# The last chunk's second product in 26 block products, and the last output row stored in two parts

## The chip, the cores and the metric

The kernel runs on one core of a Trainium2 chip. The metric is the device time of one execution in microseconds (us), as the median over runs. Traces come from one profiled execution; times in them are in us from the start of its span. Engines are named as in the profile: PE is TensorE, PEld its weight loads, DVE is VectorE, ACT is ScalarE, POOL is GpSimd, SP is SyncE, which issues most DMAs.

## The reference

Four batches, eight heads, 768 time steps and head dimension 40 go through an mLSTM cell, a recurrence with gates, whose output is rearranged to 3072 rows of 320 columns. Those go through two dense layers with a quick GELU between them:

```python
    h = x @ w_in                                  # 3072x320 @ 320x2048
    g = h * (1.0 / (1.0 + np.exp(-1.702 * h)))
    return (g @ w_out).astype(np.float32)         # 3072x2048 @ 2048x320
```

Everything is fp32. Only the end of this is touched by the change: `g @ w_out` for the last 128 time steps of all four batches, that is, for 512 rows.

## The kernel before

The time axis is cut into six chunks (`w` from 0 to 5, `NW = 6`) of 128 steps. For each chunk the cell is computed in its chunked form (scores, values, carried state); then the two dense layers follow for the chunk's 4 x 128 rows. Chunk `w`'s second layer is interleaved by hand with the cell of chunk `w + 1`, so the last chunk's second layer stands alone at the end. The order of the instructions on each engine is the order in which the program emits them (`tc.manual_schedule()`); each engine works its own queue in that order, and waits on semaphores where it needs another's result. Tiles in a pool (`bufs` of them for a tag) are used in turn.

**First layer, `up_fast` (L496).** It is called twice per chunk, for `j = 0` and `j = 4`; each call makes eight of the 16 blocks of 128 hidden units, `g`. It uses Winograd's form of Strassen's scheme (seven products of 2x2 blocks for eight) on the first 256 of the 320 inputs, and ordinary products (L546) for the other 64. Four sums of the inputs go ahead on DVE (L506 to L509); then, if given, the function `between` is called, which can emit other work to the queues at that place. PE runs the products (L518) into the banks `p_u` and `p_v`; ACT copies some out (L523); DVE adds others into `g` (L526); ACT applies the GELU (L530). L546 writes into the banks that the first four additions of L526 read, so it comes after them.

**Second layer, `down_fast` (L602).** For the chunk's rows of two batches at a time (`c` 0 and 1) it uses the same scheme once more: the hidden dimension is cut in two halves of eight blocks, the output columns in two halves of 160 (`DH`), the rows in two batches. Each of its seven products is a chain of eight hidden blocks into one PSUM bank of `ps_m` (L615); each fp32 block shows as two matmul records in the trace. DVE copies a product (L618) or adds it (L620) into the output tile `o_sb`. The sums of weights that it needs, `t1`, `t2`, `t4` and a changed `w01`, are made once, in chunk 1 (`weight_sums`, L585). The sums of hidden blocks are made per chunk by `hidden_sums` (L596) on DVE, in the room of `big` and `xs`; some in place in `g`. A row block of 128 x 320 is stored with one DMA on SP's queue when both its halves are final (L624).

The driver loop runs `up_fast(w, 0)`, then `up_fast(w, 4)`, with hidden sums emitted after each, and then the list of 14 second-layer products. At the end of the last chunk nothing else is left: POOL has nothing to do there at all.

Names that the change uses: `k_st`, `v_st`, `state`, `q_bl`, `k_bl`, `eo` and the `wt`, `kT`, `qT` tiles belong to the cell and are free once chunk 5's cell is done. `ps_a` has four PSUM banks, `ps_x` two and `ps_m` two. `V`, `A`, `G`, `T` are DVE, ACT, POOL and PE.

Of the kernel before, what the change touches and what calls it, by code (L numbers as in the profile page):

```python
# [22 lines left out]
L = 128  # L23
# [11 lines left out]
def kernel(  # L35
# [24 lines left out]
    DH = DM // 2  # L60
# [25 lines left out]
    eo = {}  # L86
# [409 lines left out]
    def up_fast(w, j, between=None):  # L496

        x = xT[w].rearrange("p c b t -> p c (b t)")  # L500
        ts = slice(0, W // 2), slice(W // 2, W)
        b00, b10, b01, b11 = (x[:, c, t] for t in ts for c in range(2))
        bt1, bt2, bt4 = (xs[:, i * 256:(i + 1) * 256] for i in range(3))
        js = range(j, j + 4)
        if j == 0:
            V.tensor_tensor(out=bt1, in0=b01, in1=b00, op=OP.subtract)  # L506
            V.tensor_tensor(out=bt2, in0=b11, in1=bt1, op=OP.subtract)
            V.tensor_tensor(out=b01, in0=b11, in1=b01, op=OP.subtract)
            V.tensor_tensor(out=bt4, in0=b10, in1=bt2, op=OP.subtract)  # L509
        if between:  # L510
            between()
        chain = {k: (ps_m if k - j < 2 else ps_x).tile([128, W], FP, tag="mx"[(k - j) // 2], name="p_u") for k in js}
        other = {k: ps_a.tile([128, W], FP, tag="a", name="p_v") for k in js}
        g = {k: hidden_of(w, k) for k in js}

        def product(p, t, a, b, first=False):
            for k in js:
                T.matmul(p[k][:, ts[t]], a[:, k // 2, k % 2 * 128:(k % 2 + 1) * 128], b, start=first,  # L518
                         stop=True, skip_group_check=True)

        def take(i, t):
            for k in js:
                A.copy(out=g[k][i][:, ts[t]], in_=chain[k][:, ts[0]])  # L523

        def add(k, i, t, p, pt):
            V.tensor_tensor(out=g[k][i][:, ts[t]], in0=p[k][:, ts[pt]], in1=g[k][i][:, ts[t]], op=OP.add)  # L526

        def gelu(k, i, t, src=None):
            dst = g[k][i][:, ts[t]]
            A.activation(out=dst, in_=dst if src is None else src, func=AF.Gelu_apprx_sigmoid)  # L530

        product(chain, 0, a00, b00, True)
        take(0, 0)
        product(other, 0, a01, b10, True)
        product(chain, 0, as2, bt2)
        take(0, 1)
        product(other, 1, as4, b11)
        product(chain, 0, a10, b01)
        take(1, 1)
        product(chain, 1, as1, bt1)  # L540
        for k in js:
            add(k, 0, 1, chain, 1)
        for k in js:
            for i, p in enumerate((other, chain)):
                r = slice(i * 64, i * 64 + 64)
                T.matmul(p[k], w_in_x[r, k, :], x[r, 2, :], start=False, stop=True, skip_group_check=True)  # L546

        for k in js:
            add(k, 1, 1, chain, 1)
            add(k, 0, 0, other, 0)  # L550
# [83 lines left out]

    def attention(w):
        if w > 1:

            return [[(columns, w)], [(weights, w, 0), (weights, w, 1)],  # L640
                    [(scores, w, 0), (hidden_sums, w - 1, 1, range(4), 3), (scores, w, 1), (weights, w, 2),
                     (weights, w, 3)],
                    [(values, w, 0), (values, w, 1), (scores, w, 2), (scores, w, 3)] +
                    [(scale, w, b) for b in (0, 1) if w + 1 < NW],
                    [(seam, w, 0), (seam, w, 1), (last_values, w)], [(carry, w)] if w + 1 < NW else [],
                    [(seam, w, 2)], [(seam, w, 3)]]
        return [[(columns, w)], [(weights, w, 0), (weights, w, 1)], [(scores, w, 0), (scores, w, 1)],
                [(weights, w, 2), (gates_out, w), (values, w, 0, 1), (scale, w, 0), (scale, w, 1)],
                [(weights, w, 3), (scores, w, 2), (scores, w, 3)], [(seam, w, 0), (seam, w, 1)],
                [(last_values, w)], [(seam, w, 2), (seam, w, 3)], [(new_states, w), (carry, w)]]  # L650
# [96 lines left out]
    def next_keys():  # L747
# [3 lines left out]
        transposes(w + 1, 0)  # L751
        transposes(w + 1, 1)

    for w in range(NW):
        more = w + 1 < NW
        for j in range(NF // 2):
            if w == 0 and j == 0:
                for pair_ in range(2):
                    for i, g in enumerate(hidden_of(0, pair_)):
                        A.activation(out=g, in_=first[pair_][i], func=AF.Gelu_apprx_sigmoid)  # L760
                    if pair_ == 0:
                        weights_in(0)
            elif w == 0 and j % 2 == 0:
                weights_in(j // 2)
                up(j, j == 2)
            elif w and j % 4 == 0:
                up_fast(w, j, next_keys if more and j == 0 else None)
            if w == 0 and j == 0:
                load_blocks(1, 0)
                spread(1)  # L770
                load_blocks(1, 1)
            if w == 1 and j == 3:
                weight_sums(3)
            if more:
                if w and j == 0:
                    load(w + 1, "o")
                if j == 4:
                    load(w + 1, "v")
                    if w:
                        spread(w + 1)  # L780
                    else:
                        fetch(17)
                        load(1, "o")
                if j == (4 if w else 6):
                    load(w + 1, "k")
                if w and j == 3:
                    for b in range(2, 4):
                        transposes(w + 1, b)
            if w and j in (3, 7):
                hidden_sums(w, 0, (j // 4 * 2, j // 4 * 2 + 1), 1, 2)  # L790
                if j == 3:
                    hidden_sums(w, 0, (0, 1), 3, 4)
        side = attention(w + 1) if more else []
        if w == 0:

            blocks = [(lambda b=b, n=n: down(w, b, n)) for ns in ((0, 1), (2,), (3,)) for b in range(B) for n in ns]
            stops = (0, 1, 5, 6, 8, 10, 12, 14, 15)
        else:
            blocks = down_fast(w, 0) + down_fast(w, 1)
            stops = (0, 1, 2, 4, 8, 10, 11, 12)  # L800
        for i, block in enumerate(blocks):
            if w == 0:
                weights_in(4 + i)
                if i == 0:
                    load_gates(2)
                if i == 2:
                    for b in range(B):
                        transposes(1, b, slice(0, 1))
                    first_sums((0, 1))
                    for b in range(B):  # L810
                        transposes(1, b, slice(1, 2))
                if i == 10:
                    load_blocks(2)
            elif w + 2 < NW and i == 0:
                load_gates(w + 2)
                load_blocks(w + 2)
            block()
            if i in stops and side:
                run(side.pop(0))
            if w == 1 and i == 1:  # L820
                weight_sums(2)
            if w:
                for at, c, *what in ((0, 0, (2, 3), 3), (1, 0, (2, 3), 4), (1, 1, range(4), 1),
                                     (5, 1, range(2), 2), (6, 1, range(2, 4), 2), (7, 1, range(4), 4)):
                    if i == at:
                        hidden_sums(w, c, *what)
                if i == 2 and not more:
                    hidden_sums(w, 1, range(4), 3)
            elif i == 11:
                weight_sums(0)  # L830
                weight_sums(1)
# [30 lines left out]
```

## Time and profile before

| what | value |
|---|---|
| median of 12 runs | 485.89 us |
| lowest and highest run | 485.77 and 486.84 us |
| the profiled execution, own time | 485.89 us |
| its span | 484.2 us |
| PE busy in the span | 478.1 us (99%) |
| DVE busy | 343.0 us (71%) |
| ACT busy | 220.7 us (46%) |
| POOL busy | 60.5 us (12%) |
| last chunk's first layer on PE | 418.65 to 450.75 us |
| last chunk's second layer on PE | 450.75 to 481.19 us |
| last DVE addition ends, last store is issued | 481.53, 481.56 us |

The busy time of PE is the modelled occupancy of a pipelined engine. The shares are averages over the whole span; the change touches the stages from 418.65 us on, and the first of them is where work of the second is prepared. DVE's and POOL's shares in those stages are what counts, not their shares of the span.

### The profile page before, as it was taken

How to read it: one execution, taken by the hardware profiler on the slowest of the kernel's cores; microseconds unless marked ns; L12 is line 12 of the kernel's file. 1: busy time of each engine (PE TensorE's matmuls, PEld its weight loads, DVE VectorE, ACT ScalarE, POOL GpSimd, SP SyncE). 2: the span in 40 equal slices, each digit the busy share in tenths (PEclk: the TensorE clock that was granted, in tenths of full speed). 3: DMA queues.
4: the chain of work that ended last, by engine and by line, in shares of the span. 5: the costliest groups of instructions: out<-in, count | busy, mean ns of one | idle time of the engine just before them, and what ended most of it. 6: DMA issues, size and time to landing. Idle time of an engine off the chain costs nothing. (4 is left out here: it accounts for less than half of the span.)

```text
span 484.2 us, 10432 instructions
## 1 busy us (share of the span) xinstructions
PE 478.1 (99%) x4072; PEld 396.9 (82%) x4072; DVE 343.0 (71%) x853; ACT 220.7 (46%) x575; POOL 60.5 (12%) x101
## 2 busy tenths in 40 slices
PE   8999999999999999999999999999999999999997
PEld 5874457777879999788999877999877999977997
DVE  8788878887978965667766677686576786254831
ACT  7667673603649302467600466900374920255300
POOL 3020001520001420000341000332000120000000
PEclk9999999999999999999999999999999999999999
DMA  9999689954997000997000896200492000000000
GB/s 127 190 257 343 86 199 198 165 76 73 194 174 79 7 30 28 213 156 81 3 29 15 124 248 66 29 28 3 85 260 22 1 15 16 28 1 0 1 27 28
DMA packets 175953, 44.87 MB, mean 93 GB/s; under 512 B 164352, under 2 KB 169504, under 8 KB 175904
## 3 DMA queue, kind: packets, MB, share of 16 engines
q1 hardware_dynamic: 175328, 43.55, 49.1%
q8 instruction: 32, 0.52, 0.5%
q10 hardware_dynamic: 576, 0.66, 0.4%
q14 instruction: 17, 0.14, 0.1%
HBM read 40.17 MB, written 4.01 MB: 91 GB/s over the span
## 5 line engine op out<-in xcount | busy, mean ns | idle before, releaser
L615 PE MATMUL p_out<-w_out_sb,g 128*128 128x160 f32 x480 | 69.8, 301 | 0.0
L615 PEld LDWEIGHTS p_out<-w_out_sb,g 128*128 128x128 f32 x480 | 66.3, 190 | 0.9
L405 ACT COPY xT<-p_x 128x384 f32<-128x384 f32 x24 | 10.8, 484 | 120.2 <-PE p_x L404 107.1
L526 DVE TENSOR_TENSOR g<-p_u,g 128x256 f32<-128x256 f32 x80 | 33.7, 424 | 44.6 <-PE p_u L518 35.0
L523 ACT COPY g<-p_u 128x256 f32<-128x256 f32 x120 | 43.1, 377 | 43.5 <-PE p_u L518 39.3
L530 ACT ACTIVATE g<-g 128x256 f32<-128x256 f32 x120 | 42.3, 424 | 39.3 <-DVE g L526 39.3
L336 POOL TENSOR_SCALAR_AFFINE_SELECT wt<-wt 128x1024 f32<-128x1024 f32 x20 | 22.8, 1138 | 239.8 <-ACT wt L334 239.0
L620 DVE TENSOR_TENSOR o_sb<-o_sb,p_out 128x160 f32<-128x160 f32 x70 | 21.4, 318 | 42.2 <-PE p_out L615 41.8
L334 ACT ACTIVATE wt<-wt,cols 128x128 f32<-128x128 f32 x160 | 47.8, 392 | 0.0
L518 PE MATMUL p_u<-xT,w_in_sb 128*128 128x256 f32 x160 | 38.9, 382 | 0.0
L518 PE MATMUL p_u<-xs,big 128*128 128x256 f32 x160 | 37.9, 379 | 0.0
L546 PE MATMUL p_v<-xT,w_in_x 64*128 64x512 f32 x80 | 37.0, 602 | 0.0
L546 PE MATMUL p_u<-xT,w_in_x 64*128 64x512 f32 x80 | 37.0, 602 | 0.0
L566 PE MATMUL p_out<-w_out_sb,g 128*128 128x320 f32 x128 | 36.3, 437 | 0.0
L352 DVE TENSOR_TENSOR wt<-p_s,wt 128x512 f32<-128x512 f32 x48 | 30.4, 683 | 8.1 <-POOL wt L336 6.7
L615 PE MATMUL p_out<-t,big 128*128 128x160 f32 x240 | 35.5, 301 | 0.0
L518 PEld LDWEIGHTS p_u<-xT,w_in_sb 128*128 128x128 f32 x160 | 29.6, 190 | 5.4 <-DVE o_sb L620 1.5
L518 PEld LDWEIGHTS p_u<-xs,big 128*128 128x128 f32 x160 | 30.0, 190 | 4.6 <-ACT g L523 0.2
L615 PEld LDWEIGHTS p_out<-t,big 128*128 128x128 f32 x240 | 33.3, 190 | 0.2
L566 PEld LDWEIGHTS p_out<-w_out_sb,g 128*128 128x128 f32 x128 | 23.7, 190 | 9.9 <-issue 0.5
L526 DVE TENSOR_TENSOR g<-p_v,g 128x256 f32<-128x256 f32 x80 | 29.8, 415 | 0.0
L546 PEld LDWEIGHTS p_v<-xT,w_in_x 64*128 64x128 f32 x80 | 14.2, 186 | 16.0 <-issue 16.0
(172 smaller groups left out, 857.4 us busy)
## 6 DMA issues: line engine op xcount, KB each, us to landing
wt<-m_row SPq DMA_DIRECT2D x20, 512.0 KB, 6.7
v_st<-in_v_dram SPq DMA_DIRECT2D x5, 640.0 KB, 8.9
eo<-in_o_gate_dram SPq DMA_DIRECT2D x5, 640.0 KB, 5.5
k_st<-in_k_dram SPq DMA_DIRECT2D x5, 640.0 KB, 11.3
out_dram<-o_sb SPq DMA_DIRECT2D x20, 160.0 KB, 1.8
big<-in_moe_w_in_dram SPq DMA_DIRECT2D x5, 512.0 KB, 7.0
k_bl<-in_k_dram SPq DMA_DIRECT2D x40, 64.0 KB, 2.7
q_bl<-in_q_dram SPq DMA_DIRECT2D x40, 64.0 KB, 2.6
```

The costliest lines, as they stand in the source:

```text
L334: A.activation(out=x[:, h, :], in_=x[:, h, :], func=AF.Exp, scale=-1.0, bias=cols[w][:, b * H + h:b * H + h + 1])
L336: G.affine_select(out=x, in_=x, compare_op=OP.is_ge, fill=0.0, base=0, pattern=[[0, H], [1, L]], channel_multiplier=-1)
L352: V.tensor_tensor(out=wt[w, b][:, :, i, :], in0=pw[i], in1=wt[w, b][:, :, i, :], op=OP.mult)
L405: A.copy(out=xT[w][:, :, b, :], in_=px)
L518: T.matmul(p[k][:, ts[t]], a[:, k // 2, k % 2 * 128:(k % 2 + 1) * 128], b, start=first, stop=True, skip_group_check=True)
L523: A.copy(out=g[k][i][:, ts[t]], in_=chain[k][:, ts[0]])
L526: V.tensor_tensor(out=g[k][i][:, ts[t]], in0=p[k][:, ts[pt]], in1=g[k][i][:, ts[t]], op=OP.add)
L530: A.activation(out=dst, in_=dst if src is None else src, func=AF.Gelu_apprx_sigmoid)
L546: T.matmul(p[k], w_in_x[r, k, :], x[r, 2, :], start=False, stop=True, skip_group_check=True)
L566: T.matmul(po, gs[w, f // 2][:, f % 2, b * L:(b + 1) * L], w_out_sb[:, f, :], start=(f == 0), stop=(f == NF - 1))
L615: T.matmul(po, a(f), b[:, f, :], start=(f == 0), stop=(f == NH - 1))
L620: V.tensor_tensor(out=dst, in0=x, in1=po, op=OP.add)
```

## The change

In the last chunk alone, `down_fast` and `hidden_sums` are not used any more. The second layer is instead cut into 4 x 4 blocks of the left matrix (four batches by four groups of four hidden blocks) and 4 x 2 blocks of the right one (four groups of hidden blocks by two column halves). A direct form takes 32 block products, two applications of the scheme before take 28 (14 products of twice the depth); the new scheme takes 26. It needs other sums of weights and of hidden blocks, and each product goes into one or two outputs with a sign; where several outputs share products, the products accumulate in one PSUM bank (a "chain"), and are read between two of them.

- `last_weights`, called as `between` of `up_fast(5, 0)`: 8 sums of weight blocks on DVE and 13 on POOL, of 128 x 640 elements each, into room that the cell has left, and into places of `t1`, `t2`, `t4` and `w_out_sb` that are free by then.
- `early_sums`, called as `between` of `up_fast(5, 4)`: the sums of hidden blocks that use only the first call's `g` (`a_early`). A sum of two blocks of `g` is two instructions of 256 columns; a sum of two earlier sums is one of 512.
- `down_last`: the 26 products in a written order; before each of them one or two of the remaining sums (`a_next`, `a_late`) are emitted to DVE; after each, DVE or ACT brings the product into its outputs. ACT does those in which an output receives its first product after the third step.
- Stores: batches 3, 1 and 0 with one DMA each; batch 2 in two, its right half ahead and its left half, which becomes final last, with a DMA of 160 columns.

The core of the diff:

```diff
+    def last_weights():
...
+        form(V, 16, b[2, 0], b[0, 0], sub)
+        form(V, 6, b[0, 0], b[3, 0], sub)
+        form(V, 8, b[1, 0], b[3, 0], sub)
+        form(V, 1, b[1, 0], wf[16], sub)
+        form(V, 18, b[1, 1], t3[0], sub)
+        form(V, 9, b[1, 1], wf[16], sub)
+        form(V, 17, b[1, 0], b[2, 0], add)
+        form(V, 2, wf[18], b[3, 1], sub)
+        form(G, 23, b[3, 1], t3[1], sub)
+        form(G, 4, wf[18], b[1, 1], add)
+        form(G, 4, wf[4], wf[23], sub)
+        form(G, 7, b[1, 1], b[3, 1], sub)
+        form(G, 26, b[1, 0], b[1, 1], sub)
+        form(G, 10, t1_[1], wf[26], sub)
+        form(G, 20, wf[26], b[2, 0], add)
+        form(G, 12, t1_[0], t1_[1], sub)
+        form(G, 13, t1_[0], b[2, 0], add)
+        form(G, 11, b[3, 0], t3[1], sub)
+        form(G, 15, wf[18], b[3, 0], sub)
+        form(G, 14, b[1, 1], b[3, 0], sub)
+        form(G, 22, b[3, 1], b[3, 0], sub)
...
+    a_early = [(9, (1, 0), (3, 1), ADD), (17, (2, 1), (3, 1), ADD), (16, (2, 0), (3, 1), ADD),
+               ("d", (1, 0), (1, 1), SUB), (24, "d", 17, ADD), (26, (3, 1), "d", SUB), (26, (0, 1), 26, ADD),
+               (25, 17, (2, 0), SUB)]
+    a_next = [(21, (0, 0), (0, 1), ADD), (19, (0, 0), (3, 0), ADD), (18, (2, 0), (3, 0), ADD)]
...
+    def down_last():
...
+        steps = [(6, None, (0, 0), "+00 -30"), (8, None, (0, 1), "+00 -10"), (1, 6, (3, 1), "-10 +30"),
+                 (4, 4, (1, 0), "-31"), (9, 5, None, "+10"), (17, 1, None, "+20"), (16, 3, None, "-20"),
+                 (2, None, (3, 3), "+01 -31"), (3, None, (0, 2), "-00 +20"), (5, 2, (2, 3), "+21"),
+                 (7, None, (1, 3), "+01 -11"), (10, 4, None, "+11"), (20, 1, None, "+21"), (12, 5, None, "-21 +31"),
+                 (13, 3, None, "-21"), (11, 2, None, "+20"), (18, 3, None, "+31"), (15, None, None, "+01 +30"),
+                 (19, 3, None, "+30"), (24, 1, None, "+11"), (14, None, None, "+01 +10"), (26, 1, None, "+10"),
+                 (21, 2, None, "-00"), (23, 4, None, "+21"), (22, 2, None, "-01"), (25, 6, None, "-20")]
+        stores = {19: (3, 0, 2), 26: (1, 0, 2), 23: (2, 1, 2), 22: (0, 0, 2), 25: (2, 0, 1)}
+        for i, (n, chain, block, takers) in enumerate(steps):
+            if i < 3:
+                a_form(*a_next[i])
+            else:
+                for _ in range(2 if i in (4, 6, 8, 10) else 1):
+                    if late:
+                        a_form(*late.pop(0))
+            p, first = bank(chain)
+            for f in range(4):
+                a = a_block(*block, f // 2)[:, f % 2, :] if block else af[n][:, f, :]
+                T.matmul(p, a, wf[n][:, f, :], start=(first and f == 0), stop=(f == 3), skip_group_check=True)
+            for taker in takers.split():
...
+                    V.tensor_tensor(out=dst, in0=dst, in1=p, op=ADD if taker[0] == "+" else SUB)
...
+            if n in stores:
+                b, c0, c1 = stores[n]
+                nc.sync.dma_start(out=out[b * S + w * L:b * S + (w + 1) * L, c0 * DH:c1 * DH],
+                                  in_=o[b][:, c0 * DH:c1 * DH])
...
-                up_fast(w, j, next_keys if more and j == 0 else None)
+                up_fast(w, j, (next_keys if j == 0 else None) if more else last_weights if j == 0 else early_sums)
...
-            if w and j in (3, 7):
+            if more and w and j in (3, 7):
                 hidden_sums(w, 0, (j // 4 * 2, j // 4 * 2 + 1), 1, 2)
...
-        side = attention(w + 1) if more else []
+        if not more:
+            down_last()
+            break
+        side = attention(w + 1)
```

A step of `steps` names the product, its chain (`None`: a bank of its own in `ps_m`; 5 and 6 in `ps_x`; the others in `ps_a`), the block of `g` it reads (`None`: a sum), and the outputs it goes into, each as sign, batch and column half.

More of the change, by code (lines that the diff above doesn't have):

```diff
@@ L632, in down_fast, with w_block, a_block, room_for_weights @@
                 lambda: (product(summed(2), w11, (o01, o01)), store(0))]
+    last = NW - 1
+    quarter = (0, NH, 4, NH + 4)
+    wf, af = {}, {}
+    def w_block(k, n):
+        return w_out_sb[:, quarter[k]:quarter[k] + 4, n * DH:(n + 1) * DH]
+    def a_block(b, k, two):
+        return gs[last, quarter[k] // 2 + two][:, :, b * L:(b + 1) * L]
+    def room_for_weights(t, n):
+        flat = t.rearrange({3: "p a b -> p (a b)", 4: "p a b c -> p (a b c)"}[len(t.shape)])
+        return [flat[:, i * 4 * DH:(i + 1) * 4 * DH].rearrange("p (f m) -> p f m", m=DH) for i in range(n)]
@@ new lines, in last_weights, with form @@
+    def last_weights():
+        free_v = room_for_weights(k_st, 3) + room_for_weights(v_st, 2) + room_for_weights(state, 2)
+        wt_room = work.tile([L, NP, 2, L], FP, tag="wt", bufs=4, name="wt")
+        free_g = (room_for_weights(q_bl, 3) + room_for_weights(k_bl, 3) + room_for_weights(eo[last], 2) +
+                  room_for_weights(wt_room, 1) + room_for_weights(t2, 2) + [t4[:, 0:4, :]])
+        b = {(k, n): w_block(k, n) for k in range(4) for n in range(2)}
+        t3 = [b[0, 1], b[2, 1]]
+        t1_, t4_ = ([t[:, i * 4:i * 4 + 4, :] for i in range(2)] for t in (t1, t4))
+        def form(E, name, x, y, f):
+            if name not in wf:
+                wf[name] = (free_v if E is V else free_g).pop(0)
+            E.tensor_tensor(out=wf[name], in0=x, in1=y, op=f)
+        add, sub = OP.add, OP.subtract
+        wf.update({3: t4_[1], 5: t3[1], 18: t3[0], 19: t1_[0], 21: b[3, 0], 24: b[1, 1], 25: b[2, 0]})
+        form(V, 16, b[2, 0], b[0, 0], sub)
[19 more added lines that the diff above has]
+        form(G, 22, b[3, 1], b[3, 0], sub)
@@ new lines, in room_for_hidden, with a_form @@
+    def room_for_hidden(t):
+        flat = t.rearrange("p a b c -> p (a b c)") if len(t.shape) == 4 else t
+        return [flat[:, i * 4 * L:(i + 1) * 4 * L].rearrange("p (f t) -> p f t", t=L) for i in range(2)]
+    free_a = []
+    def a_form(name, x, y, f, neg=False):
+        if not free_a:
+            for tag in ("kT", "qT"):
+                free_a.extend(work.tile([128, NP, L], FP, tag=tag, bufs=4, name=tag) for _ in range(4))
+            for i in range(3):
+                free_a.extend(room_for_hidden(big[:, i, :]))
+            for _ in range(3):
+                free_a.extend(room_for_hidden(work.tile([L, NP, 2, L], FP, tag="wt", bufs=4, name="wt")))
+            for i in range(3, 6):
+                free_a.extend(room_for_hidden(big[:, i, :]))
+        ops = [lambda two, v=v: a_block(*v, two) if isinstance(v, tuple) else af[v][:, 2 * two:2 * two + 2, :]
+               for v in (x, y)]
+        whole = not isinstance(x, tuple) and not isinstance(y, tuple)
+        ins = [(af[x], af[y])] if whole else [(ops[0](two), ops[1](two)) for two in range(2)]
+        if name not in af:
+            af[name] = free_a.pop(0)
+        for two, (in0, in1) in enumerate(ins):
+            dst = af[name] if whole else af[name][:, 2 * two:2 * two + 2, :]
+            if neg:
+                V.scalar_tensor_tensor(out=dst, in0=in0, scalar=-1.0, in1=in1, op0=OP.mult, op1=f)
+            else:
+                V.tensor_tensor(out=dst, in0=in0, in1=in1, op=f)
@@ new lines @@
+    ADD, SUB = OP.add, OP.subtract
+    a_early = [(9, (1, 0), (3, 1), ADD), (17, (2, 1), (3, 1), ADD), (16, (2, 0), (3, 1), ADD),
+               ("d", (1, 0), (1, 1), SUB), (24, "d", 17, ADD), (26, (3, 1), "d", SUB), (26, (0, 1), 26, ADD),
+               (25, 17, (2, 0), SUB)]
+    a_next = [(21, (0, 0), (0, 1), ADD), (19, (0, 0), (3, 0), ADD), (18, (2, 0), (3, 0), ADD)]
+    a_late = [(10, (1, 0), (1, 2), ADD), (20, 10, 17, SUB), (12, (1, 0), (3, 2), SUB), (13, (3, 2), (2, 0), SUB),
+              (11, (2, 3), (0, 2), SUB), (18, 18, (3, 3), ADD), (15, (0, 0), (3, 3), SUB),
+              (19, 19, (3, 2), SUB, True), (24, (1, 3), 24, SUB), (14, (0, 1), (1, 3), SUB), (26, 26, (1, 2), SUB),
+              ("x", (0, 3), (2, 3), ADD), (21, 21, "x", SUB, True), (23, (2, 2), (2, 3), ADD),
+              (23, 23, (3, 2), ADD), (23, 23, 10, SUB), (22, 21, 11, ADD), ("x", 14, 15, ADD), (22, 22, "x", ADD),
+              ("d", (0, 2), (2, 2), ADD), (25, 25, "d", SUB)]
@@ new lines, in down_last, with bank @@
+    def down_last():
+        w = last
+        o = [op.tile([128, DM], FP, tag="o", name="o_sb") for _ in range(2)]
+        o += [work.tile([L, H, D1], FP, tag="u", name="u").rearrange("p h d -> p (h d)")[:, 0:DM] for _ in range(2)]
+        begun, banks = set(), {}
+        late = list(a_late)
+        def bank(chain):
+            if chain in banks:
+                return banks[chain], False
+            pool, tag = (ps_m, "m") if chain is None else (ps_x, "x") if chain in (5, 6) else (ps_a, "a")
+            p = pool.tile([128, DH], FP, tag=tag, name="p_out")
+            if chain is not None:
+                banks[chain] = p
+            return p, True
+        steps = [(6, None, (0, 0), "+00 -30"), (8, None, (0, 1), "+00 -10"), (1, 6, (3, 1), "-10 +30"),
[6 rows of a table added]
+        stores = {19: (3, 0, 2), 26: (1, 0, 2), 23: (2, 1, 2), 22: (0, 0, 2), 25: (2, 0, 1)}
+        for i, (n, chain, block, takers) in enumerate(steps):
+            if i < 3:
+                a_form(*a_next[i])
+            else:
+                for _ in range(2 if i in (4, 6, 8, 10) else 1):
[6 more added lines that the diff above has]
+            for taker in takers.split():
+                b, half_ = int(taker[1]), int(taker[2])
+                dst = o[b][:, half_ * DH:(half_ + 1) * DH]
+                if (b, half_) in begun:
+                    V.tensor_tensor(out=dst, in0=dst, in1=p, op=ADD if taker[0] == "+" else SUB)
+                elif i < 3:
+                    V.tensor_scalar(out=dst, in0=p, scalar1=1.0 if taker[0] == "+" else -1.0, scalar2=None,
+                                    op0=OP.mult)
+                else:
+                    A.activation(out=dst, in_=p, func=AF.Copy, scale=1.0 if taker[0] == "+" else -1.0)
+                begun.add((b, half_))
+            if n in stores:
+                b, c0, c1 = stores[n]
+                nc.sync.dma_start(out=out[b * S + w * L:b * S + (w + 1) * L, c0 * DH:c1 * DH],
+                                  in_=o[b][:, c0 * DH:c1 * DH])
@@ L752, in next_keys, with early_sums @@
         transposes(w + 1, 1)
+    def early_sums():
+        for x in a_early:
+            a_form(*x)
     for w in range(NW):
@@ L826 @@
                         hidden_sums(w, c, *what)
-                if i == 2 and not more:
-                    hidden_sums(w, 1, range(4), 3)
             elif i == 11:
```

## The prediction

> **What bounds the kernel now.** I read the busy line first, then the chain, the stages, the waits and single instructions. The chain of waits ends with two pieces:
>
> ```profile
> 450.75 30.44 PE p_out L615 x224
> 481.19 0.02 issue
> 481.21 0.32 DVE o_sb L620
> ```
>
> The last chunk's second product is TensorE and nothing else: 224 matmuls in 30.44 us, 0.1359 us each, with no gap between products. Whatever removes a matmul here moves the end, if the vector side keeps up. The stages (columns: stretch, its length, then busy us and count of PE, PEld, DVE, ACT and POOL) say how much vector time is free:
>
> ```profile
> 418.65:434.72 16.07, 16.07 (x73) 11.81 (x73) 7.48 (x21) 7.97 (x20) 0.00 (x0) 1.00 0.03 12
> 434.72:450.75 16.03, 16.03 (x75) 12.01 (x74) 9.00 (x25) 9.32 (x29) 0.00 (x0) 1.00 0.00 0
> 450.75:481.20 30.45, 30.43 (x224) 30.18 (x223) 13.46 (x42) 2.88 (x10) 0.00 (x0) 1.00 0.05 17
> ```
>
> PE fills all three stages (the two halves of the last up product, then the down product). DVE is about half idle; POOL does nothing after 411 us. The waits of the up product show where DVE's free time lies:
>
> ```profile
> DVE g L526 <- PE p_u L518: 13.5, 2, 7.5
> ```
>
> DVE waits twice for L518's product, 7.5 us (420.47 to 428.00) and 6.0 us (437.97 to 443.93). The additions (L526) that follow gate PE: L546 writes the banks they read. By the timeline the first addition ends at 428.42 where L546 comes at 429.19, and at 444.36 against 445.13: slack 0.77 us both times. Work put into the two waits is free only while it ends within about 0.8 us of them.
>
> [...] L596 with both inputs in SBUF, minimum, median and maximum in ns, and a contested stretch in time order:
>
> ```profile
> L596 DVE TENSOR_TENSOR big<-xs,g x20: 410/416/884, 169.0 to 466.6; 128x256 f32<-128x256 f32 x20
> L411 POOL TENSOR_TENSOR v_st<-v_st,cols x20: 735/736/1178, 25.0 to 329.1; 128x328 f32<-128x328 f32 x20
> ```
> ```profile
> 91.67 0.99 POOL L411 TENSOR_TENSOR v_st<-v_st,cols 128x328 f32<-128x328 f32 x1
> ...
> 92.11 1.11 DVE L235 SCALAR_TENSOR_TENSOR w_out_sb<-big,w_out_sb 128x512 uint32<-128x512 uint32 x1
> ...
> 92.63 1.18 POOL L417 TENSOR_TENSOR state<-state,cols 128x328 f32<-128x328 f32 x1
> ...
> 93.35 1.00 DVE L237 CUSTOM_DVE_ANT_0 w_out_sb<-big,w_out_sb 128x1024 uint16<-128x1024 uint16 x1
> 93.77 1.18 POOL L411 TENSOR_TENSOR v_st<-v_st,cols 128x328 f32<-128x328 f32 x1
> ```
>
> They take turns: one DVE instruction per POOL instruction, each starting in effect 0.14 us before the other's end. That matters, since the change gives POOL 13 additions. [...]
>
> **The change, part by part.**
> *PE.* 26 products of 4 blocks for 14 of 8: 208 matmuls for 224, the same shapes: 16 x 0.1359 = 2.17 us less, 28.27 us.
>
> *Unit costs.* DVE addition start to start: 256 columns 0.335 (four in 1.43, one 0.42), 160 columns 0.235, so 1.04 ns a column and 0.07; 512: 0.60; 640: 0.735. One that needs the instruction just ahead: 0.11 more. POOL at 640 columns: the select at L336 (1.087 for 1024) and one at L206 (0.292 for 128) give 0.18 fixed and 0.887 ns a read; two reads fit the 0.735 (0.18 + 328 x 2 x 0.887 = 0.76). An estimate for 640: 1.28 us[...]. I take 1.28 and keep 1.23 to 1.45.
>
> *First wait, weight forms.* DVE gets 8 of 640 columns from 420.39. The first five run alone to 424.15. POOL's second form needs the fifth, so it starts there; the last three DVE forms then alternate with two POOL forms and end at 428.45 instead of about 426.3. The L526 additions start 0.45 late, inside the 0.77. Cost to PE: nothing; the cover is that slack, and it is gone beyond 1.4 us per POOL form, at up to 0.2.
>
> *Second wait, early sums.* The 8 sums of L596 go; 15 instructions come (14 of 256, one of 512), which need the GELUs that ACT ends at 437.1 to 437.7. Alone they take 14 x 0.335 + 0.60 + 0.11 = 5.4 and end at 442.8, before 443.93: free. But POOL has 10 forms left at 428.45. At 1.235 start to start it ends its seventh at 437.17; three are left, and each lets one DVE sum by: 438.27, 439.69, 441.11. Then POOL is done at 441.25, and twelve DVE instructions (4.73) end at 445.84. The first addition behind them ends at 446.3, where PE wanted it at 445.13: **PE waits 1.2 us**. The same walk with 1.23 per form: 0.6; with 1.33: 1.6;[...] with 1.45: 2.9. If POOL's first form doesn't run in its idle time before 420, another 1.1.
>
> *Last stage.* DVE gets 21 sums in 35 instructions (28 of 256, 7 of 512), 6 more at the start, and 31 accumulations of 160 columns (ACT takes 4): 34 x 0.335 + 7 x 0.60 + 0.7 + 31 x 0.235 = 23.6 us beside 28.3 of PE, where DVE was busy 13.5 (24 sums of L596 and 18 reads of products go). Sums are made at least five products ahead, so PE never waits for one. But DVE is a queue, and each accumulation stands behind a sum. Products 3 to 18 put about 18 us of DVE beside 16.3 of PE (15 x 1.087), so it falls behind by about 0.9 us near product 14. Where a bank is used again two products later (the chain of products 13, 18, 19), PE waits: walked through product by product, 0.45 us in sum. DVE 3% dearer gives 0.8, 7% gives 1.5; bounds 0.2 and 1.5; I take 0.6. ACT's 4 copies are free (2.88 us busy there).
>
> *Stores.* Four become five on SP, 0.33 us of issue each; the last three are 1.09 us apart, so none queues. The last store is 80 KB for 160:
>
> ```profile
> out_dram<-o_sb SPq DMA_DIRECT2D x20, 160.0 KB, 1.8
> m_row<-m_run SPq DMA_DIRECT2D x5, 16.0 KB, 1.4
> ```
>
> Between these, 80 KB lands about 0.22 earlier (0.4 x 80/144); bounds 0 and 0.35. Take 0.2.
>
> *Sum*: -2.17 + 0 + 1.2 + 0.6 - 0.2 = -0.57 us. The profiled execution took 485.89 (span 484.2 and 1.7 around it), which is also the median: **485.3 us**.
>
> **Rivals.**
> *No contention (faster).* If POOL's forms are done by 437 (about 1.1 us each, or started earlier), the early sums fit: -2.17 + 0.45 - 0.2 = -1.9, 484.0. For it: the local fit was made from shapes other than the one used. Against it: the exclusion shows in three L596 at 0.88 and in the stretch above, and POOL can't start before DVE's fifth form. 0.30.
> *The new wait outgrows the saving (slower).* One mechanism: early sums behind POOL's forms, in front of L546 at 445. At 1.45 per form[...] 2.9 us: -2.17 + 2.9 + 0.6 - 0.2 = +1.1, 487.0; with the first form late too, 488. It passes +0.97 where PE's wait reaches about 2.75. For it:[...] the tight last stage can only add. 0.34.
> *The change doesn't do what it says:* if the blocks were split into more matmuls or products had gaps, PE would show more than 208 x 0.1359. No boundary between products costs anything now, so I give it nothing of its own.
>
> **How the numbers follow.** A measurement of this kernel tells about 0.2% (0.97 us) from no change. The middle case has 0.36, with a range of its own of 484.9 to 486.6[...]. Faster 0.30, slower 0.34. The range to hold the time 8 times in 10 reaches over most of both: 483.8 to 487.8.
>
> **What would show it.** After the change the last stage should hold 208 PE matmuls in 28.3 to 29.8 us; POOL should show 13 additions of 640 columns, from which the rest follows; early sums should start singly, one per POOL form, then run on; PE should have one gap at L546 near 445 of 0.6 to 2.9 us, and short gaps at the chain of 13, 18 and 19. A gap of nothing at 445 with POOL still busy at 438 would refute the exclusion; a gap elsewhere, or a PE wait for a sum or a weight form, would refute my reading of the order. Losses spread over all products of the last stage would mean that DVE bounds it.

## The result, and the profile after

The changed kernel takes 490.87 us (median of 7 runs, 489.90 to 491.43) against 485.89 before: a ratio of 1.0097, 95% interval 1.0088 to 1.0106. It is 5.0 us slower. The prediction was 485.3 with a range up to 487.8; the direction forecast as likeliest, no measurable change, was wrong, and the time lies outside the range. The profiled execution took 491.06 us, its span is 489.2; the accounts below are of this one execution.

The end of the chain of waits after the change, to be held against the same three lines of before:

```profile
456.09 1.92 PE p_u L518 x8
458.01 28.34 PE p_out L769 x208
486.35 0.02 issue
486.38 0.32 DVE u L774
```

The last stage did what it was to do: 208 matmuls in 28.34 us for 224 in 30.44, 2.10 us less, without a gap. But it starts at 458.01 instead of 450.75. The stage (columns as before the change) shows DVE busy 23.4 us in it where it was 13.5:

```profile
458.01:486.35 28.34, 28.33 (x209) 28.04 (x207) 23.41 (x71) 4.38 (x15) 0.00 (x0) 1.00 0.05 16
```

Among the waits, DVE's two waits for L518 (13.5 us in sum) have shrunk to one, and PE now waits for DVE:

```profile
PE p_u L546 <- DVE g L526: 3.4, 1, 3.4
...
DVE g L526 <- PE p_u L518: 1.6, 1, 1.6
```

Further up, the same chain names who held it back:

```profile
433.60 3.35 ACT g L530 x11
436.95 0.02 issue
436.97 9.42 DVE kT L719 x8
446.39 0.02 issue
446.41 2.70 DVE qT L719 x7
449.11 0.34 DVE g L526
449.46 0.04 issue
449.50 1.22 PE p_u L546
```

L719 is here the early sums: eight sums of hidden blocks, made by 15 instructions. Below, as in the prediction, each of the 15 is called a sum. The first eight of them take 9.42 us, and would take 2.8 alone; the additions of L526 come after all 15, and PE's matmul at L546 after the first of those. POOL's work in that stretch is its forms (L665), the sums of weight blocks of `last_weights`. The timeline of POOL and DVE (start, us, engine, operation, count):

```profile
435.32 1.55 POOL L665 TENSOR_TENSOR eo<-t 128x640 f32<-128x640 f32 x1
436.82 1.54 POOL L665 TENSOR_TENSOR eo<-t,w_out_sb 128x640 f32<-128x640 f32 x1
438.33 1.72 POOL L665 TENSOR_TENSOR wt<-w_out_sb 128x640 f32<-128x640 f32 x1
440.01 5.08 POOL L665 TENSOR_TENSOR t<-w_out_sb 128x640 f32<-128x640 f32 x3
```
```profile
436.97 9.41 DVE L719 TENSOR_TENSOR kT<-g 128x256 f32<-128x256 f32 x8 [2.08 <-ACT g L530]
```

Five POOL forms overlap the sums, one at a time. The first of them was running when the first sum came, and lasts 1.54 us as alone; the other four meet a sum each and last 1.72. Five of the sums last 1.68 to 1.76 us instead of 0.42, with no wait recorded between them. Not every DVE instruction beside POOL is longer: L526's additions, which have one input in PSUM, keep their 0.42 us between 430.23 and 433.15, where one POOL form follows the other. The group of these sums in the after trace, minimum, median and maximum in ns:

```profile
L719 DVE TENSOR_TENSOR kT<-g x10: 412/1048/1761, 437.0 to 478.5; 128x256 f32<-128x256 f32 x10
```

PE's own timeline shows the gap, and what follows it; the stages below it show the granted clock (third column from the end) in the same stretch:

```profile
444.96 1.12 PE L546 MATMUL p_v<-xT,w_in_x 64*128 64x512 f32 x2
449.50 1.22 PE L546 MATMUL p_u<-xT,w_in_x 64*128 64x512 f32 x1 [3.42 <-DVE g L526]
...
450.51 1.06 PE L546 MATMUL p_u<-xT,w_in_x 64*128 64x512 f32 x1
```
```profile
446.00:448.00 2.00, 0.09 (x1) 0.00 (x0) 1.97 (x6) 0.00 (x0) 0.00 (x0) 1.00 0.00 0
448.00:450.00 2.00, 0.50 (x2) 0.50 (x4) 2.00 (x7) 0.00 (x0) 0.00 (x0) 0.63 0.00 0
450.00:452.00 2.00, 2.00 (x6) 0.69 (x5) 0.83 (x4) 0.00 (x0) 0.00 (x0) 0.50 0.00 0
```

The first p_u matmul of L546 in the same place before the change:

```profile
445.13 0.69 PE L546 MATMUL p_u<-xT,w_in_x 64*128 64x512 f32 x1
```

After the change, in steps of half a us, the clock falls while PE still stands idle:

```profile
448.00:448.50 0.50, 0.00 (x0) 0.00 (x0) 0.50 (x3) 0.00 (x0) 0.00 (x0) 1.00 0.00 0
448.50:449.00 0.50, 0.00 (x0) 0.00 (x0) 0.50 (x2) 0.00 (x0) 0.00 (x0) 0.52 0.00 0
```

The first p_u matmul comes at 449.50; before the change it came at 445.13, with everything ahead of it 0.16 us later. That is 4.53 us of wait. From there to the start of the last stage PE takes 8.51 us (449.50 to 458.01) where it took 5.62 (445.13 to 450.75): the clock is at half from about 448.5 to 455.3, and the matmuls of L546 come 0.85 us apart instead of 0.43. That is 2.89 us more. The sum closes: 4.53 + 2.89 - 2.10 in the last stage - 0.16 in the tail (2.85 us from the last matmul to the end of the span, 3.01 before) - 0.16 ahead of all this is 5.0 us, the difference of the spans.

### The profile page after: what moved, and what is told of

It is laid out like the page before. It is cut to its first block, busy times and chain, and to the rows that moved or that the text cites. A ratio compares the mean times of both kernels' runs of the same rounds, so it can differ in the third digit from the quotient of the medians.

```text
span 489.2 us, 10478 instructions
## 1 busy us (share of the span) xinstructions
PE 480.1 (98%) x4056; PEld 396.2 (81%) x4056; DVE 367.6 (75%) x897; ACT 222.3 (45%) x580; POOL 82.6 (17%) x114
## 5 line engine op out<-in xcount | busy, mean ns | idle before, releaser
L526 DVE TENSOR_TENSOR g<-p_u,g 128x256 f32<-128x256 f32 x80 | 33.4, 424 | 35.2 <-PE p_u L518 23.2
L615 PE MATMUL p_out<-w_out_sb,g 128*128 128x160 f32 x384 | 56.1, 301 | 0.0
L615 PEld LDWEIGHTS p_out<-w_out_sb,g 128*128 128x128 f32 x384 | 53.0, 190 | 0.9
L546 PE MATMUL p_u<-xT,w_in_x 64*128 64x512 f32 x80 | 39.9, 641 | 3.4 <-DVE g L526 3.4
L546 PE MATMUL p_v<-xT,w_in_x 64*128 64x512 f32 x80 | 39.9, 639 | 0.0
L518 PE MATMUL p_u<-xT,w_in_sb 128*128 128x256 f32 x160 | 38.9, 382 | 0.0
L518 PE MATMUL p_u<-xs,big 128*128 128x256 f32 x160 | 37.9, 379 | 0.0
L620 DVE TENSOR_TENSOR o_sb<-o_sb,p_out 128x160 f32<-128x160 f32 x56 | 17.1, 317 | 26.8 <-PE p_out L615 26.4
L518 PEld LDWEIGHTS p_u<-xT,w_in_sb 128*128 128x128 f32 x160 | 29.6, 190 | 5.4 <-DVE o_sb L620 1.5
L518 PEld LDWEIGHTS p_u<-xs,big 128*128 128x128 f32 x160 | 30.0, 190 | 4.6 <-ACT g L523 0.2
L566 PEld LDWEIGHTS p_out<-w_out_sb,g 128*128 128x128 f32 x128 | 23.8, 190 | 9.8 <-issue 0.5
L526 DVE TENSOR_TENSOR g<-p_v,g 128x256 f32<-128x256 f32 x80 | 29.8, 415 | 0.0
L615 PE MATMUL p_out<-t,big 128*128 128x160 f32 x192 | 28.5, 301 | 0.0
L615 PEld LDWEIGHTS p_out<-t,big 128*128 128x128 f32 x192 | 26.6, 190 | 0.2
L546 PEld LDWEIGHTS p_v<-xT,w_in_x 64*128 64x128 f32 x80 | 14.9, 196 | 14.6 <-issue 14.6
```

The source lines that it names most:

```text
L566: T.matmul(po, gs[w, f // 2][:, f % 2, b * L:(b + 1) * L], w_out_sb[:, f, :], start=(f == 0), stop=(f == NF - 1))
L615: T.matmul(po, a(f), b[:, f, :], start=(f == 0), stop=(f == NH - 1))
L620: V.tensor_tensor(out=dst, in0=x, in1=po, op=OP.add)
```

## The experiments

Theory: the early sums wait for POOL's forms, one for one; the additions behind them hold PE; and PE's pause halves its clock. Rival A: 15 early sums are too many for that place by themselves. Rival B: L546 is slow because the additions pace it, not the clock. All times are medians, beside the kernel before on the same chip (485.75 to 485.82 us, and one run of 486.01 in the last).

**POOL's forms left out.**

```diff
         def form(E, name, x, y, f):
+            if E is G:
+                wf.setdefault(name, b[0, 0])
+                return
```

> The changed kernel with POOL's 13 weight forms left out (the products that need them read another weight block, so the output is not the reference's); everything else is in place, the 8 weight forms and 15 early sums on DVE among it. Theory (the early sums wait for POOL's forms, and the long gap on PE halves its clock): the early sums run from 437.0 to about 442.6, ahead of the additions; no gap at L546 near 445, L546 there takes 3.7 us instead of 6.6, the last stage stays at 28.3; 7.3 us less than the changed kernel, 483.5 us. Rival A (15 early sums are too many for that wait by themselves): a gap of over 1 us stays, 485 us or more. Rival B (L546 is slow because the additions pace it, not the clock): L546 stays near 6.6 us, about 486.5 us.

Measured: 483.58 us, ratio 0.9955 (0.994 to 0.997). L546 took 3.6 us (445.10 to 448.73), the last stage 28.34. Rival A falls: the same 15 sums in the same place cost nothing once POOL is quiet. L546 isn't always slow either; but the additions are on time here, so that late additions pace L546 is excluded only by the zeros in the gap, below.

**One form, then two forms, from POOL to DVE.** The second kernel moves 14 as well.

```diff
         form(V, 2, wf[18], b[3, 1], sub)
+        form(V, 22, b[3, 1], b[3, 0], sub)
...
-        form(G, 22, b[3, 1], b[3, 0], sub)
```

> POOL's last form (22) is made by DVE, as its ninth, ahead of the first additions; nothing else changes. Theory: POOL's first waits for DVE's longer run (0.7 us later) but ends 0.8 to 1.0 us earlier in all, so PE's gap falls from 4.5 (3.4 of it with PE idle) to about 3.5 us. If the halved clock comes from the length of the gap, it may not be halved any more: 487.0 us; if it is halved all the same, 489.9. Rival B expects L546 at 6.6 us whatever the gap: 489.9.

> POOL's forms 14 and 22 are made by DVE, its ninth and tenth, which just fit before the first additions. Theory: PE's gap falls by about 1.9 to 2.6 us and its clock stays full, so L546 takes 3.7 us: 486.1 us. Rival B: L546 at 6.6 us, 489.0. Rival A expects little change of the gap, since the number of early sums is the same: 490.

Measured: 489.32 us (ratio 1.0078, 1.0063 to 1.0093) and 487.95 (1.004, 1.0022 to 1.0058). The gap is smaller with each form, though by less than expected: PE idles 2.66 and 2.06 us, for 3.42 in the changed kernel, where about 1.0 us less was expected for the first form and 1.9 to 2.6 less for both.

```profile
449.17 1.22 PE L546 MATMUL p_u<-xT,w_in_x 64*128 64x512 f32 x1 [2.66 <-DVE g L526]
```
```profile
448.15 0.69 PE L546 MATMUL p_u<-xT,w_in_x 64*128 64x512 f32 x1 [2.06 <-DVE g L526]
```

The first line is of the kernel with one form moved, the second of that with two: 1.22 us for the first matmul is half clock, 0.69 is full clock (0.50 and 1.00 in the stage from 449 to 451 of each). With one form moved the clock was halved still, in all four runs, and the time is near the expectation for that (489.9); the profiled execution, at 490.51, is the longest of the four. With two, the profiled execution kept its clock and took 486.73 us. The kernel's six runs spread from 486.63 to 489.10, while the kernels without a gap stay within about 1 us. The mean clock of each run tells them apart: the three at 1.000 took 486.63 to 487.37 us, the three at 0.996 took 488.52 to 489.10.

**POOL's forms in another order.** As the kernel with two forms moved, and POOL's five forms that need nothing of DVE go ahead of form 4, which waits for DVE's form 18:

```diff
         form(G, 23, b[3, 1], t3[1], sub)
-        form(G, 4, wf[18], b[1, 1], add)
-        form(G, 4, wf[4], wf[23], sub)
         form(G, 7, b[1, 1], b[3, 1], sub)
         form(G, 26, b[1, 0], b[1, 1], sub)
         form(G, 10, t1_[1], wf[26], sub)
         form(G, 20, wf[26], b[2, 0], add)
+        form(G, 4, wf[18], b[1, 1], add)
+        form(G, 4, wf[4], wf[23], sub)
+        form(G, 15, wf[18], b[3, 0], sub)
...
-        form(G, 15, wf[18], b[3, 0], sub)
```

> As the kernel with two forms on DVE, and POOL's other 11 forms in another order: the five that need nothing of DVE first (23, 7, 26, 10, 20), which can run from 411 while DVE has little to do, then those that wait for DVE's form 18. All the work of the change is done. Theory: POOL ends its first five at 418.6, starts the others behind DVE's run at about 427.6 and is done at 436.6, before the early sums: no contention, no gap, full clock; as the kernel without POOL's forms, 483.5 us, 0.5% below the kernel before. Rival A: 485 or more.

Measured: 483.68 us, ratio 0.996 (0.9946 to 0.9974). The early sums in DVE's timeline:

```profile
437.14 0.43 DVE L719 TENSOR_TENSOR kT<-g 128x256 f32<-128x256 f32 x1 [2.08 <-ACT g L530]
437.75 2.44 DVE L719 TENSOR_TENSOR kT<-g 128x256 f32<-128x256 f32 x7 [0.18 <-ACT g L530]
...
443.94 1.72 DVE L526 TENSOR_TENSOR g<-p_u,g 128x256 f32<-128x256 f32 x4 [1.03 <-PE p_u L518]
```

Eight sums in 3.1 us, and DVE now waits 1.03 us for PE ahead of the additions, not PE for DVE. All of the change's work is in this kernel, and it is faster than the kernel before as well as the changed one. Measured a second time:

> The reordered kernel once more, with more rounds and on one chip with the kernel that stores batch 2 whole: 483.7 us, 0.43% below the kernel before, with an interval that excludes no change.

Measured: 483.58 us, ratio 0.9951 (0.9938 to 0.9965), as expected.

**Eight forms first.** The kernel just shown, with 12, 13 and 11 brought forward to stand behind 20:

```diff
         form(G, 20, wf[26], b[2, 0], add)
+        form(G, 12, t1_[0], t1_[1], sub)
+        form(G, 13, t1_[0], b[2, 0], add)
+        form(G, 11, b[3, 0], t3[1], sub)
         form(G, 4, wf[18], b[1, 1], add)
```

> As the reordered kernel (five POOL forms ahead of the wait on DVE's form 18, two of the 13 on DVE), but with eight ahead: 12, 13 and 11 come forward too, so that POOL is still busy from 418.9 on, beside DVE's four input sums (L506 to L509) and its ten weight forms. Theory of turns (one DVE instruction for one POOL instruction): the input sums run singly, the tenth DVE form ends near 431.5 instead of 427.8, the first additions are late and PE has a gap of about 2.8 us at the first L546 (429.3): 486.5 us, up to 3.7 more where the clock is halved. Rival (back-to-back DVE instructions keep POOL out, as POOL's form 4 waited for the whole run of DVE forms in every kernel so far): POOL waits instead, DVE is late by 0.3 us at most: 483.7 us.

Measured: 486.82 us (486.46 to 489.22), ratio 1.0028 (1.0014 to 1.0043). Here the four input sums of DVE meet POOL:

```profile
418.80 1.78 DVE L506 TENSOR_TENSOR xs<-xT 128x256 f32<-128x256 f32 x1
420.61 1.65 DVE L507 TENSOR_TENSOR xs<-xT,xs 128x256 f32<-128x256 f32 x1
422.18 1.76 DVE L508 TENSOR_TENSOR xT<-xT 128x256 f32<-128x256 f32 x1
423.86 0.41 DVE L509 TENSOR_TENSOR xs<-xT,xs 128x256 f32<-128x256 f32 x1
```

Three take turns with POOL's last three ahead of form 4, the fourth runs alone. The gap moves to the first half's L546: its first p_u matmul came at 432.02, after 1.41 us of idle PE. The same turns, at another place, at about the expected price (486.5): five runs kept their clock and took 486.46 to 487.02 us, three had it lowered (mean 0.996) and took 488.18 to 489.22. The sixth to eighth form cost 3.1 us in the median only because of who stands beside them.

**The early sums behind the additions.**

```diff
-                up_fast(w, j, (next_keys if j == 0 else None) if more else last_weights if j == 0 else early_sums)
+                up_fast(w, j, (next_keys if j == 0 else None) if more else last_weights if j == 0 else None)
...
         late = list(a_late)
+        early_sums()
```

> The changed kernel with the 15 early sums emitted at the start of the last stage, behind the additions of L526, instead of ahead of them; POOL's forms as in the changed kernel. Theory (the gap comes from the additions' place in DVE's queue behind sums that wait for POOL): no gap at L546 near 445, full clock, POOL's forms end uncontested near 443.5. The 5.4 us of sums now load the last stage, where DVE then has about 28.8 us for 28.3 of PE: PE waits there for banks, 2 to 4 us in sum: 486.7 us (485.5 to 488). If the gap came from POOL's forms directly (PE waiting for a weight form), it would stay, and the time with it, near 491 or above.

Measured: 489.25 us, ratio 1.0077 (1.0061 to 1.0093). The gap at L546 is gone, as the theory says, so PE doesn't wait for a weight form. The size was a miss: the stages show PE idle for a whole 3 us in the last one, and the clock halved after it.

```profile
462.00:465.00 3.00, 0.00 (x0) 0.00 (x0) 3.00 (x11) 0.00 (x0) 0.00 (x0) 1.00 0.00 0
465.00:468.00 3.00, 2.61 (x10) 2.64 (x11) 3.00 (x12) 0.00 (x0) 0.00 (x0) 0.54 0.00 0
```

I had 2 to 4 us of waits; one wait of 3.8 us came in one piece, at one bank, and the clock loss came on top. In this order of DVE's queue there is no room for these sums in the last stage.

**Zeros in the gap.** The changed kernel, with matmuls that add zeros into a bank:

```diff
+                if w == NW - 1 and k == 4 and i == 1:
+                    for _ in range(14):
+                        T.matmul(other[4], idle, idle.unsqueeze(1).to_broadcast([128, 4, 128]), start=False, stop=True,
+                                 skip_group_check=True)
                 T.matmul(p[k], w_in_x[r, k, :], x[r, 2, :], start=False, stop=True, skip_group_check=True)
```

> The changed kernel with 14 bf16 matmuls of 128x512 of zeros added into the p_v bank that PE is about to leave, ahead of the p_u matmul of L546 that waits near 445: about 3.0 us of PE work inside the gap, so PE isn't idle for longer than about 0.5 us. The gap stays as it is. Theory (the idle PE's clock is halved, which makes L546 take 6.6 us instead of 3.7): the clock stays full, 2.9 us less than the changed kernel, 488.0 us. Rival B (the additions pace L546, or the long gap is all of the loss): 490.9 us.

Measured: 488.20 us (488.14 to 488.36), ratio 1.0048 (1.0034 to 1.0063). PE's timeline:

```profile
446.15 3.19 PE L548 MATMUL p_v<-idle 128*128 128x512 bf16 x14
449.64 0.69 PE L550 MATMUL p_u<-xT,w_in_x 64*128 64x512 f32 x1 [0.29 <-DVE g L526]
```

The wait ends at 449.64, as late as in the changed kernel (449.50), but the matmul behind it takes 0.69 us instead of 1.22. The additions are as late as before and the matmuls aren't slow, so rival B falls. Work that computes nothing saves 2.7 us, close to the 2.89 of the accounting. So the halved clock is shown to be a consequence of PE's pause.

How long a pause does it? The mean granted clock of each run says whether it was lowered (0.993 to 0.997) or kept (0.999 or 1.000):

| kernel | PE idle ahead of L546, profiled execution | runs that kept the clock | runs with it lowered |
|---|---|---|---|
| changed | 3.42 us | none | 7: 489.90 to 491.43 us |
| one form moved | 2.66 us | none | 4: 488.85 to 490.51 us |
| two forms moved | 2.06 us | 3: 486.63 to 487.37 us | 3: 488.52 to 489.10 us |
| eight forms first | 1.41 us | 5: 486.46 to 487.02 us | 3: 488.18 to 489.22 us |
| changed, with zeros | 0.29 us | 4: 488.14 to 488.36 us | none |

So there is no sharp length. By the traces the clock fell 2.4 us into the pause in the changed kernel, and with eight forms first about 0.7 us after PE had gone on (the matmuls of L546 come 0.53 us apart, then 0.64, then 0.85); with one form moved it was at half when PE went on (first matmul 1.22 us). What decides it besides the pause, no run here shows.

**The store alone**, on the kernel before, and **the reordered kernel without it**:

```diff
-                lambda: product(block(0, 1), w10, (o00, o00)),
+                lambda: (product(block(0, 1), w10, (o00, o00)), store(0, 0, 1) if split else None),
...
-                lambda: (product(summed(2), w11, (o01, o01)), store(0))]
+                lambda: (product(summed(2), w11, (o01, o01)), store(0, 1, 2) if split else store(0))]
```
```diff
-        stores = {19: (3, 0, 2), 26: (1, 0, 2), 23: (2, 1, 2), 22: (0, 0, 2), 25: (2, 0, 1)}
+        stores = {19: (3, 0, 2), 26: (1, 0, 2), 22: (0, 0, 2), 25: (2, 0, 2)}
```

> The kernel before with one part of the change alone: in the last chunk, batch 2's left half is stored after the second product of its group, and its last store has 160 columns. By the tail of the changed kernel (2.85 us from PE's last matmul to the end of the span against 3.01): 0.16 us less than the kernel before, 485.6 us; the prediction's figure was 0.2. Rival (one more DMA late costs as much as it gives): no difference.

> The reordered kernel with batch 2 stored by one DMA of 320 columns at the end, so without the first part of the change. By the split store alone on the kernel before (0.08 us, which the interval doesn't tell from nothing): 0.1 to 0.2 us more than the reordered kernel, 483.8 us.

Measured: 485.72 us beside 485.80 (ratio 0.9998, 0.9989 to 1.0006), and 483.75 beside 483.58 with the split store. The differences are 0.08 and 0.17 us. Both point the way that was expected, and neither tells a gain from nothing.

**Who gets in when: forms that arrive during a run.** In the changed kernel and in the reordered one, form 4 had waited for the whole rest of DVE's run of weight forms (3.53 and 5.00 us long in the traces). Three POOL forms were moved behind an early sum, by a POOL copy that reads it:

```diff
+        def late_forms():
+            G.tensor_copy(out=free_g[-1][:, 0, 0:1], in_=af[9][:, 0, 0:1])
+            form(G, 12, t1_[0], t1_[1], sub)
+            form(G, 13, t1_[0], b[2, 0], add)
+            form(G, 11, b[3, 0], t3[1], sub)
```

> The reordered kernel with its last three POOL forms (12, 13, 11) moved behind the first early sum, on which a small POOL copy waits, so that POOL is idle until DVE's run of early sums has begun. If a POOL instruction that arrives during a run of back-to-back DVE instructions waits for the end of that run (form 4 waited 2.0, 2.7 and 3.5 us for the rest of the runs of weight forms): form 12 starts in effect near 440.1, where sum 24 waits for the one ahead of it, and lasts over 3 us in the trace; then turns, three contests in all: the early sums end near 446, PE has a gap of 2 to 4 us at L546. If turns hold from the first instruction on, form 12 lasts about 1.8 us from 438.3, each of the three forms delays one sum, and the early sums end near 446 as well. The time tells the two apart little (485.5 to 490 us); the trace does.

Measured: 485.71 us in one run, and turns from the first form on (1.74, 1.72, 1.72 us from 437.63). So a form that arrives during a run of sums gets in. PE was idle for 1.1 us here and kept its clock (mean 0.999); for the time, one run says little. Then each weight form of DVE was made by two instructions of 320 columns:

```diff
-            E.tensor_tensor(out=wf[name], in0=x, in1=y, op=f)
+            if E is V:
+                for h in range(2):
+                    r = slice(2 * h, 2 * h + 2)
+                    E.tensor_tensor(out=wf[name][:, r, :], in0=x[:, r, :], in1=y[:, r, :], op=f)
+            else:
+                E.tensor_tensor(out=wf[name], in0=x, in1=y, op=f)
```

> The reordered kernel with each of DVE's ten weight forms made by two instructions of 320 columns instead of one of 640: 20 x 0.40 = 8.0 us of DVE for 7.35, so the first additions are some 0.6 us late, inside their slack, and the time stays near 483.7 us. In all kernels so far POOL's form 4 waited for the whole rest of the run of 640-column forms (5.0 us in the trace in the reordered kernel), while it took turns with runs of 256-column sums. If the length of DVE's instructions makes the difference, form 4 now gets in between two of them and lasts about 1.9 us, and takes turns with the rest, which makes DVE later: the additions start near 430.5 or later, PE has a gap at the first L546 of 1 us or more. If it is something else (the strided blocks of w_out_sb, or POOL's first instruction after a wait), form 4 lasts about 5.5 us and the time is 483.7.

Measured: 484.39 us in one run, no gap at L546, and form 4 waits out the whole run again:

```profile
425.27 5.34 POOL L670 TENSOR_TENSOR k_bl<-w_out_sb 128x640 f32<-128x640 f32 x1 [5.65 <-DVE w_out_sb L668]
```

So halving the length of DVE's instructions changes nothing. Whether it is the blocks of `w_out_sb` that both engines read, or POOL's first large instruction after a wait, stays open; it doesn't bear on the result.

## Why the prediction was wrong, point by point

- **PE's saving**: 2.17 us forecast, 2.10 measured. Right.
- **First wait**: "Cost to PE: nothing". Right in its outcome, wrong in its path. I had DVE's last three forms alternate with POOL; instead DVE ran them without a break (the last two from 424.65 to 426.20) and POOL's form 4 waited, 3.53 us long in the trace. So the additions had more room than I gave them, and POOL started its queue of ten at 429.18 instead of 428.4, nearer to the early sums.
- **Second wait**: this step failed, by its size: 1.2 us forecast, 4.53 measured. The mechanism was the forecast one, down to the order of events: sums singly, one for each POOL form, then a run, then the late additions. The term that was mis-sized is POOL's form: "An estimate for 640: 1.28 us" measured 1.54. I fitted it to an addition whose second operand is a broadcast (L411, 0.735 us for 328). That two full operands cost more is the difference I see, but no run isolates it; the strided weight blocks aren't the reason, since forms with none (`q_bl<-q_bl`) took 1.54 as well. The upper end of my range, 1.45, is shown by no trace of before; the 0.735 us for 328, taken in proportion to the columns, give an estimate of 1.43 for 640, still below the measured 1.54. With 1.54 my own walk through both waits gives an estimate of 4.0 us, where I had 1.2 and the rival 2.9. POOL's start, another 0.2 us later in the trace, and PE's own, 0.16 us earlier, are most of what is left up to 4.53. Five forms were left at 437, not three.
- **What was left out**: the clock, which the sum has at nothing, without a reason. I named a gap of 0.6 to 2.9 us on PE and gave it only its own length. The trace shows half clock (0.50 in the stages above): it fell 2.4 us into the pause of the changed kernel, and it fell in three of eight runs of the kernel whose profiled execution had 1.41 us of idle PE. This term was worth 2.89 us in the profiled execution, more than the whole saving of 2.10.
- **Last stage**: 0.6 us of bank waits forecast, 0.07 measured (28.34 against 208 x 0.1359 = 28.27). DVE was as busy as I said (23.4 us in that stage, 23.6 forecast). It did fall behind, as forecast: its addition of the eleventh product starts at 471.13, 1.1 us after PE's end of that product (470.0, by equal steps of 1.09), and it is half a us behind at the fourteenth. But PE waited for no bank. Which entry of my walk was too dear isn't shown.
- **Stores**: 0.2 us forecast, 0.16 in the tail of the trace; the runs don't tell it from zero.
- **The rivals**: the slower one was right in its mechanism ("early sums behind POOL's forms, in front of L546 at 445"), and the wait passed its mark of 2.75 us by far. Its 487.0 still had POOL too cheap (1.45 us a form for a measured 1.54) and lacked the clock. The faster one is what the reordered kernel then made true: 484.0 forecast for it, 483.6 measured.

## What to carry to other kernels

Before additions are handed to POOL because it is idle, look at which DVE instructions with two SBUF inputs will run beside them, and what waits behind those in DVE's queue: with turns, a sum of 0.42 us took 1.68 to 1.76 beside POOL's forms of 1.54, while additions with one input in PSUM kept their 0.42. Emit first what needs nothing of the other engine; in this kernel the order of POOL's forms and two of them given to DVE turned +1.0% into -0.4 to -0.5%. When a step puts a pause like those here (1.41 to 3.42 us of idle PE) on PE, price the lowered clock after it too (2.89 us in the changed kernel), and take a duration from a row with the same kind of operands (1.54 us measured here, for 1.28 from another kind).

## What was not expected of the hardware

- A POOL addition of two full fp32 operands, 128 x 640, took 1.54 us alone; one with a broadcast operand, 128 x 328, 0.735. Per column beyond a fixed 0.18 us (an estimate from the selects, 1.087 us for 1024 and 0.292 for 128) that is 2.1 ns against 1.7.
- Turns between DVE and POOL aren't the only outcome: with runs of DVE's weight forms, POOL's waiting instruction lasted 3.53 us for 3 forms left (changed kernel) and 5.00 for 5 (reordered), and 5.34 when they were cut in halves.
- PE's clock was halved in some or all runs of the four kernels whose profiled execution had 1.41 to 3.42 us of idle PE ahead of L546 (table above), and in the changed kernel it fell 2.4 us into the pause, before that was over. It stayed at half for 3.4 us with eight forms first (by the spacing of the matmuls) and with the sums behind the additions (by its stages), and for 6.8 us in the changed kernel. Fourteen bf16 matmuls of zeros in the pause kept it at full in all four runs (mean 1.000).
